# The last six row tiles of w2 straight into the result's bank, in four transfers, with the residual added by a matmul

## The chip, the cores and the metric

One core of one Trainium2 chip runs the kernel; the other cores stand idle. The metric is the device time of one execution in microseconds (us), and kernels are compared by the median of several executions. Beside that there is one profiled execution, whose trace gives a start and a duration for each instruction on each engine: PE is TensorE's matmul, PEld its weight load, DVE is VectorE, ACT ScalarE, POOL GpSimd, and SP the engine that issues the transfers here.

## The reference

One decode step of a parallel transformer block, for two sequences (B = 2) with one new token each, all in fp32. The layer norm of x feeds two branches, and the result is their sum with x:

```python
# x: (2, 1, 1024); k_cache, v_cache: (2, 4, 32768, 128)
# wq: (1024, 4096); wo: (4096, 1024); w1: (1024, 3584); w2: (3584, 1024)
xn = layernorm(x)
q = xn @ wq                                  # 32 query heads of 128, 4 key heads
p = softmax(q @ k.T * 128 ** -0.5)           # over 32768 cached positions
attn = (p @ v) @ wo
mlp = silu(xn @ w1) @ w2
return x + attn + mlp
```

Nearly all of the data are the two caches (2 x 4 x 32768 x 128 numbers each, 268 MB together) and the four weights; with two tokens, hardly any number read is used more than a few times.

## The kernel before

**The stream.** Everything large passes once through two SBUF buffers, `buf[0]` and `buf[1]`, of 128 partitions x 16384 fp32, 8 MiB each. `load` (line 169) issues a transfer on SP's queue, after a wait until the buffer's previous contents have been used. There are 40 steps (`STEPS`), alternating between the buffers: wq in two, w1 in two, then eight turns (4 key heads x 2 sequences) of two K halves and two V halves, then wo in two and w2 in two. All transfers come from SP in program order, so they stand in one queue.

**The matmuls of a step.** `slots(k, banks)` (line 300) works off a buffer with its 32 weights of 32 columns, `wt[k]`. A step is 32 matmul calls with 512 columns each; call (bank, r, q) goes to the 32 output partitions of column group q in one of two PSUM banks, and r = 0..3 accumulate. `ps[0]` and `ps[1]` are two banks each and together make `xy`. In fp32 a call shows as two matmul rows in the trace. A loop, `te_loop` (line 331), does a step on buffer A and then the first bank of a step on buffer B; a branch leads to `te_more` (line 338), which does the second bank and goes on to `te_k` or `te_v` and back, or, in the last of the 20 pairs, to `te_rest`. The semaphores `ld` (transfer landed) and `tok` (weights ready) are taken ahead of a step. `more[0]` and `more[1]` let a step wait for a second transfer in its middle: the last step of each buffer comes in pieces, and all other steps find enough counts there from the start (line 323).

**w2.** w2 has 28 row tiles of 128 rows x 1024 columns. The first sixteen go into buffer A in two transfers. The last twelve, tiles 0 to 11 in what follows, go into buffer B, in seven transfers (lines 185 to 187): tiles 0-5, tiles 6-7, tile 8, tile 9, tile 10, and tile 11 in a part with three quarters of each group's columns (`CUT`, 192 of 256) and one with the last quarter. Tiles 0 to 7 are worked off by `slots(1, (0,))` into the first bank of `ps[1]`: each r covers two tiles in halves of 512 columns, and r = 3, tiles 6-7, waits for `more[1]`. Tiles 8 to 11 go straight into `acc`, the bank of the result, by `tile` and `quarter` (lines 397 to 403): for each tile four calls of 256 columns, one per column group, on the semaphores `last[0]` to `last[4]`.

**How the result comes together.** ScalarE copies the banks of wo's two steps and w2's first step into `ev[0]` to `ev[2]` (line 254). POOL adds `ev[1]`, then x (`xs[:64, 256:768]`, line 380), then `ev[2]` (line 382); VectorE adds the two halves of that into `rest` (line 384), and then adds the first bank of `ps[1]` (line 386), which it may read after the PE semaphore's first mark, put on tile 8's last matmul. That gives `ob`, announced by `tob`. TensorE folds `ob` into `acc` with two matmuls against `fold` (lines 407 to 409), between tile 9 and tile 10. After tile 11, ScalarE copies `acc` to `ot` (line 256) and SP sends it out (line 389).

**What sets the order.** It is written out by hand: each engine runs its own instructions in program order, and semaphores tie them together. Matmuls all carry line 107 (the helper `mm`), transfers into the buffers line 172.

Of the kernel before, what the change touches and what calls it, by code (L numbers as in the profile page):

```python
# [8 lines left out]
B, HQ, HKV, SK, DH, D, F = 2, 32, 4, 32768, 128, 1024, 3584  # L9
P = 128  # L10
REP = HQ // HKV
W = 16384
NC = SK // W
KT = D // P
FT = F // P
QW = D // 4
CUT = 3 * QW // 4
LOOPS = HKV * B
STEPS = 4 + 4 * LOOPS + 4
PAIRS = STEPS // 2  # L20
# [31 lines left out]
def gqa_plus_mlp_kernel(nc, x8, kt, v0, v1, wq, wo, w1a, w1b, w2a, w2b, out):  # L52


    pe, dve, act, pool = (Stream(nc, e, n) for e, n in
                          ((nc.tensor, "pe"), (nc.vector, "dve"), (nc.scalar, "act"), (nc.gpsimd, "pool")))
    sp, T, V, A, G = nc.sync, nc.tensor, nc.vector, nc.scalar, nc.gpsimd
    sems = [pe.sem, dve.sem, act.sem, pool.sem]

    def sem(name):  # L60
        sems.append(nc.alloc_semaphore(name))
        return sems[-1]

    def sb(name, *shape):
        return nc.alloc_sbuf_tensor(name, shape, F32).ap()

    def bank(name, n=512):
        return nc.alloc_psum_tensor(name, (P, n), F32).ap()

    buf = [sb(n, P, W) for n in ("bufA", "bufB")]  # L70
    ld, more, tok = ([sem(f"{n}{k}") for k in "AB"] for n in ("ld", "more", "tok"))
    ldx, turn_sem = (sem(n) for n in ("ldx", "marks"))
    freed, subbed, normed, tq, pself = (sem(n) for n in ("freed", "subbed", "normed", "tq", "pself"))
    trm, tgd, tls, tob = (sem(n) for n in ("trm", "tgd", "tls", "tob"))
    last = [sem(f"last{i}") for i in range(5)]
    done = sem("done")

    weights, st = sb("weights", P, 64, 32), sb("st", P, 2048)
    wt = [weights[:, :32], weights[:, 32:]]
    xs, xT = sb("xs", P, D), sb("xT", P, KT, 32)  # L80
    stats, mv, ln = sb("stats", P, 2, V.BN_STATS_DIM), sb("mv", P, 2), sb("ln", P, 6)
    ev = [sb(f"ev{i}", P, 1024) for i in range(4)]
    sumq, sumh = sb("sumq", P, 1024), sb("sumh", P, FT * 32)
    tqs, qall = sb("tqs", P, 32, 32), sb("qall", P, LOOPS, REP)
    pre, sig, rsig = sb("pre", P, FT, 32), sb("sig", P, FT, B), sb("rsig", P, FT, B)
# [4 lines left out]
    def zeroed(*shape):  # L90
        n = shape[0] * (shape[1] if len(shape) > 1 else 1)
        lo = used[0]
        used[0] += n
        t = blank[:, lo:lo + n]
        return t.rearrange("p (a m) -> p a m", m=shape[1]) if len(shape) > 1 else t

    ident, sel, fold, rm, lsum, gd, ob = (zeroed(n) for n in (P, 32, 160, REP, REP, REP, 512))
    oT, hT = zeroed(HQ, 32), zeroed(FT, 32)
# [3 lines left out]
    ps = [xy[:, :1024], xy[:, 1024:]]  # L102
    smA, smB = bank("smA"), bank("smB")
    acc = bank("acc")[:, :QW]

    def mm(o, lhsT, rhs, start=True, stop=True):
        return T.matmul(o, lhsT, rhs, start=start, stop=stop)  # L107
# [13 lines left out]
    t = pool.mark(G.affine_select(out=ident, in_=ident, compare_op=ALU.not_equal, fill=1.0, base=0,  # L121
                                  pattern=[[-1, P]], channel_multiplier=1))
    pool.wait(t)
    halves = fold[:, 32:].rearrange("p (a m) -> p a m", m=64)[:, :, :32]
    t = pool.mark(G.tensor_add(halves, *(ident[:, 64 * g:64 * g + 64].rearrange("p (a m) -> p a m", m=32)
                                         for g in range(2))))
# [6 lines left out]
    for i in range(2):  # L133
        t = dve.mark(V.bn_stats(stats[:, i, :], xs[:, i * 512:(i + 1) * 512]))
    dve.wait(t)
    t = dve.mark(V.bn_aggr(mv, stats))
    var, std, y0, t0, t1, rstd = (ln[:, i:i + 1] for i in range(6))
    dve.wait(t)
    t = dve.mark(V.tensor_scalar_add(var, mv[:, 1:2], EPS))
    act.wait(t)  # L140
    t = act.mark(A.activation(std, var, AF.Sqrt))
    for f in (lambda: V.reciprocal(y0, std),
# [6 lines left out]
        t = dve.mark(f())  # L149
# [16 lines left out]
    def step(n):  # L166
        return (turn_sem, n) if n <= 2 else (freed, n - 2)

    def load(k, dst, src, s, n):
        if n:  # L170
            sp.wait_ge(*step(n))
        sp.dma_start(buf[k][:, dst] if isinstance(dst, slice) else dst, src).then_inc(s, 16)  # L172
# [3 lines left out]
    load(1, every, w1a, ld[1], 2)  # L176
    for it in range(LOOPS):
        h, b = divmod(it, B)
# [2 lines left out]
    load(0, every, wo[0], ld[0], STEPS - 5)  # L181
    load(1, every, wo[1], ld[1], STEPS - 4)
    load(0, slice(0, W // 2), w2a[:, :W // 2], ld[0], STEPS - 3)
    load(0, slice(W // 2, W), w2a[:, W // 2:], more[0], 0)
    cuts = [0, 6 * D, 8 * D, 9 * D, 10 * D, 11 * D, 11 * D + 4 * CUT, 12 * D]
    for lo, hi, s in zip(cuts, cuts[1:], [ld[1], more[1], *last]):
        load(1, slice(lo, hi), w2b[:, lo:hi], s, STEPS - 2 if lo == 0 else 0)


    for n in range(4):  # L190
        act.wait(step(n + 1))
        if n == 2:
            A.copy(ev[n][:, :512], ps[0][:, :512])
            A.copy(ev[n][:64, 512:], ps[0][:64, 512:])
            t = act.mark(A.copy(ev[n][64:96, 512:], ps[0][96:, :512]))
        else:
            t = act.mark(A.copy(ev[n], ps[n % 2]))
# [9 lines left out]
        elif n == 2:  # L207
            t = pool.mark(G.tensor_add(sumh[:96, 512:], a[:96, :384], b[:96, :384]))
            for j in range(3):
                pool.wait(t)  # L210
                t = pool.mark(G.tensor_add(sumh[96:, 512 + P * j:512 + P * (j + 1)], a[32 * j:32 * j + 32, 384:],
                                           b[32 * j:32 * j + 32, 384:]))
# [14 lines left out]
    t = dve.mark(V.transpose(pre.rearrange("p t m -> p (t m)"), sumh))  # L227

    act.wait(t)
    t = act.mark(A.activation(sig, pre[:, :, ::16], AF.Exp, scale=-1.0))  # L230
    for f in (lambda: V.tensor_scalar_add(sig, sig, 1.0), lambda: V.reciprocal(rsig, sig),
              lambda: V.tensor_mul(hT[:, :, ::16], pre[:, :, ::16], rsig)):
        dve.wait(t)
        t = dve.mark(f())
# [5 lines left out]
           tqs[:, :, ::16].rearrange("p (h m) b -> p h b m", m=REP)).then_inc(tq, 1)  # L240
    for it in range(LOOPS):
        h, b = divmod(it, B)
# [54 lines left out]
            m.then_inc(tok[c], 1)  # L297
        G.sem_inc(pself, -1)

    def slots(k, banks):  # L300

        m = None
        for bk in banks:
            for r in range(4):
                if (k, bk, r) in ((0, 1, 0), (1, 0, 3)):
                    pe.take(more[k], 16)
                for q in range(4):
                    e = 16 * bk + 4 * r + q
                    n = 16 * bk + 4 * q + r if k == 0 else e
                    m = mm(ps[k][32 * q:32 * q + 32, bk * 512:(bk + 1) * 512], wt[k][:, e, :],  # L310
                           buf[k][:, n * 512:(n + 1) * 512], r == 0, r == 3)
        return m

    def taken(k):
        pe.take(ld[k], 16)
        pe.take(tok[k])
# [3 lines left out]
    T.reg_mov(pair, 0)  # L320
    T.reg_mov(half, 0)
    pe.wait(i_const)
    for s, n in ((trm, 1), (tgd, 1), (tls, 1), (tob, 1), (more[0], 16 * PAIRS - 16), (more[1], 16 * PAIRS - 16)):
        T.sem_inc(s, n)
    T.br("te_loop")

# [4 lines left out]
    with nc.body("te_loop", valid_engines=engine):  # L331
        again = T.mark_branch_hint_location()
        taken(0)
        slots(0, (0, 1)).then_inc(turn_sem, 1)
        taken(1)
        slots(1, (0,))
        T.br_eq(pair, PAIRS - 1, on_true="te_rest", on_false="te_more")
    with nc.body("te_more", valid_engines=engine):
        slots(1, (1,)).then_inc(turn_sem, 1)
        T.reg_add(pair, pair, 1)  # L340
        T.br_eq(half, 0, on_true="te_k", on_false="te_v")
    with nc.body("te_k", valid_engines=engine):
# [6 lines left out]
    with nc.body("te_v", valid_engines=engine):  # L349
# [4 lines left out]
        for r in range(4):  # L354
            m = mm(smB[:, :REP], ob[:, r * P:(r + 1) * P], sel[:, REP * r:REP * (r + 1)], r == 0, r == 3)
        m.then_inc(turn_sem, 1)
        T.br("te_loop").branch_hint(again)
    with nc.body("turns", valid_engines=[V.engine, G.engine]):
        for eng, f, reg, step in turns:
            f()  # L360
            eng.reg_add(reg, reg, step)
            eng.br_lt(reg, step * LOOPS, on_true="turns", on_false="te_rest")
    nc.switch_bb("te_rest")
# [7 lines left out]
        G.tensor_copy(wt[c].rearrange("p (t d) m -> p t d m", d=2),  # L371
                      oT[:, 16 * c:16 * c + 16, None, :].to_broadcast([P, 16, 2, 32])).then_inc(tok[c], 1)
    pool.wait(i_hT)
    for c, n in enumerate((16, 8)):
        pool.wait(outs[c])
        G.tensor_copy(wt[c][:, :2 * n].rearrange("p (t d) m -> p t d m", d=2),
                      hT[:, 16 * c:16 * c + n, None, :].to_broadcast([P, n, 2, 32])).then_inc(tok[c], 1)
    t = pool.mark(G.tensor_add(ev[0], ev[0], ev[1]))
    pool.wait(t)
    t = pool.mark(G.tensor_add(ev[0][:64, :512], ev[0][:64, :512], xs[:64, 256:768]))  # L380
    pool.wait(t, outs[2])
    t = pool.mark(G.tensor_add(ev[0], ev[0], ev[2]))  # L382
    dve.wait(t)
    t = dve.mark(V.tensor_add(rest, ev[0][:, :512], ev[0][:, 512:]))  # L384
# [9 lines left out]
    sp.wait_ge(done, 16)  # L394
    sp.sem_inc(done, -16)

    def quarter(o, lhsT, w, start=False, stop=False):
        return [mm(o[32 * j:32 * j + 32, :], lhsT[j], w[j], start, stop) for j in range(4)][-1]

    def tile(t, o, lo, n, start=False, stop=False):  # L400
        T.wait_ge(last[t], 16)
        at = buf[1][:, lo:lo + 4 * n].rearrange("p (j n) -> p j n", j=4)
        return quarter(o, [hT[:, min(24 + t, FT - 1), :]] * 4, [at[:, j] for j in range(4)], start, stop)

    pe.mark(tile(0, acc, 8 * D, QW, True))
    tile(1, acc, 9 * D, QW)
    T.wait_ge(tob, 1)
    for c in range(2):
        mm(acc, fold[:, 32 - 32 * c:160 - 32 * c], ob[:, c * QW:(c + 1) * QW], False, False)
    tile(2, acc, 10 * D, QW)  # L410
    tile(3, acc[:, :CUT], 11 * D, CUT)
    pe.mark(tile(4, acc[:, CUT:], 11 * D + 4 * CUT, QW - CUT, False, True))


# [54 lines left out]
```

## Time and profile before

| | us |
|---|---|
| median of 3 runs | 772.55 |
| lowest and highest of them | 772.29 and 772.61 |
| profiled execution, its own time | 772.44 |
| span of its trace, first to last instruction | 771.1 |
| PE busy within the span | 392.9 |
| DVE, POOL, ACT busy | 133.3, 44.2, 29.0 |

The profiled execution spends 1.34 us around the span, so a time read from the trace stands to the execution's own time by that. Times in the trace count from the first instruction of the span. The mean granted TensorE clock was 0.752 of full speed. In rows of the timeline the first number is the start, the second the time that the group takes from first start to last end, "x" the number of instructions in the group, and the brackets say how long the engine was idle before and what released it. "PEq" is TensorE's own sequencer, "issue" idle time for which the profile shows no wait.

### The profile page before, as it was taken

The page shows a single profiled execution, that of the slowest core. Times are in us where ns is not written, and L with a number is a line of the kernel's source. Part 1 is how long each engine was busy: PE and PEld are TensorE (multiplying, and loading weights), DVE is VectorE, ACT ScalarE, POOL GpSimd, SP SyncE. Part 2 cuts the span into 40 slices and gives each one's busy share as a digit, 9 for nine tenths or more (in the row PEclk, how much of TensorE's full clock was granted, in tenths as well). Part 3 has the DMA queues.
Part 4 walks back from the last instruction along what each step waited for, and adds up shares of the span by engine and source line. Part 5 has one row for each costly group of instructions (what it writes and reads, how often), then busy time and mean ns, then how long its engine had stood idle before and what let it go on. Part 6 is the DMA issues. An engine that isn't in the chain of part 4 may idle for free. (4 is left out here: it accounts for less than half of the span.)

```text
span 771.1 us, 6114 instructions
## 1 busy us (share of the span) xinstructions
PE 392.9 (51%) x2702; PEld 125.9 (16%) x2702; DVE 133.3 (17%) x100; ACT 29.0 (4%) x39; POOL 44.2 (6%) x65
## 2 busy tenths in 40 slices
PE   0454554464545454645464545454645455545476
PEld 0111111121112111211121112111211121112122
DVE  2000104030403030304030303031303030313000
ACT  0000100100010001000100010001000100010000
POOL 3001200001000000010001000100010001000121
PEclk9977667767677767677767677767677767677689
DMA  9999999999999999999999999999999999999997
GB/s 382 435 435 435 435 435 435 435 435 435 435 435 435 435 435 435 435 435 435 435 435 435 435 432 435 425 428 418 425 432 435 432 435 435 435 435 435 435 433 329
DMA packets 6816, 331.40 MB, mean 430 GB/s; under 512 B 776, under 2 KB 920, under 8 KB 1440
## 3 DMA queue, kind: packets, MB, share of 16 engines
q1 hardware_dynamic: 6800, 331.37, 99.5%
q10 hardware_dynamic: 16, 0.03, 0.0%
HBM read 331.38 MB, written 0.02 MB: 430 GB/s over the span
## 5 line engine op out<-in xcount | busy, mean ns | idle before, releaser
L107 PE MATMUL xy<-bufB,weights 128*32 128x512 f32 x1248 | 181.8, 747 | 166.6 <-PEq L49 166.6
L107 PE MATMUL xy<-bufA,weights 128*32 128x512 f32 x1280 | 178.2, 718 | 100.4 <-PEq L49 100.4
L107 PEld LDWEIGHTS xy<-bufB,weights 128*32 128x32 f32 x1248 | 49.7, 134 | 298.8 <-issue 298.7
L107 PEld LDWEIGHTS xy<-bufA,weights 128*32 128x32 f32 x1280 | 49.9, 129 | 212.1 <-issue 212.1
L268 DVE STREAM_TRANSPOSE st<-xy 128x2048 f32<-128x2048 f32 x8 | 18.5, 2317 | 241.5 <-PE xy L107 241.5
L278 DVE TENSOR_REDUCE blank<-xy 128x512 f32<-128x2048 f32 x8 | 18.3, 2292 | 224.5 <-PE xy L107 224.5
L290 POOL MEMSET weights<- 128x2048 f32 x8 | 14.4, 1805 | 526.9 <-POOLq L49 526.9
L107 PE MATMUL smA<-blank 128*8 128x128 f32 x20 | 5.4, 370 | 51.9 <-PEq L49 51.9
L107 PE MATMUL smA<-blank,ones 128*128 128x8 f32 x18 | 4.9, 347 | 50.6 <-PEq L49 50.6
L269 DVE TENSOR_REDUCE blank<-st 128x8 f32<-128x2048 f32 x8 | 30.5, 3808 | 0.3
L279 DVE TENSOR_REDUCE blank<-weights 128x8 f32<-128x2048 f32 x8 | 30.4, 3798 | 0.0
L245 ACT ACTIVATE weights<-st 128x1024 f32<-128x1024 f32 x16 | 16.0, 1048 | 326.6 <-DVE st L275 326.6
L275 DVE TENSOR_TENSOR st<-st,gmax 128x2048 f32<-128x2048 f32 x8 | 18.3, 2292 | 0.3
L107 PE MATMUL smB<-blank 128*128 128x8 f32 x72 | 15.9, 349 | 0.0
L107 PEld LDWEIGHTS smB<-blank 128*128 128x128 f32 x72 | 15.6, 317 | 0.0
L107 PEld LDWEIGHTS smA<-blank,ones 128*128 128x128 f32 x18 | 4.3, 298 | 58.5 <-issue 58.5
L248 ACT COPY blank<-onew 128x8 f32<-128x8 f32 x8 | 1.6, 204 | 279.4 <-DVE onew L282 279.4
L107 PEld LDWEIGHTS smA<-blank 128*8 128x8 f32 x20 | 1.3, 89 | 60.2 <-issue 60.2
L384 DVE TENSOR_TENSOR rest<-ev 128x512 f32<-128x512 f32 x1 | 0.7, 693 | 49.1 <-POOL ev L382 49.1
L296 POOL COPY weights<-qall 128x128 f32 x32 | 8.0, 295 | 3.1 <-POOL weights L290 3.1
L107 PE MATMUL smB<-blank,ones 8*128 8x8 f32 x20 | 5.3, 333 | 5.7 <-PEq L49 5.7
L222 DVE STREAM_TRANSPOSE tqs<-sumq 128x1024 f32<-128x1024 f32 x1 | 1.2, 1245 | 38.2 <-POOL sumq L206 38.2
(59 smaller groups left out, 59.4 us busy)
## 6 DMA issues: line engine op xcount, KB each, us to landing
bufA<-in_w2a SPq DMA_DIRECT2D x2, 4096.0 KB, 24.0
bufA<-in_w1b SPq DMA_DIRECT2D x1, 6144.0 KB, 24.8
bufB<-in_w2b SPq DMA_DIRECT2D x1, 3072.0 KB, 16.5
bufB<-in_w2b SPq DMA_DIRECT2D x3, 512.0 KB, 20.2
bufB<-in_w2b SPq DMA_DIRECT2D x1, 1024.0 KB, 18.6
bufB<-in_w2b SPq DMA_DIRECT2D x1, 384.0 KB, 21.5
bufA<-in_kt SPq DMA_DIRECT2D x8, 27.7
bufB<-in_kt SPq DMA_DIRECT2D x8, 28.9
```

The lines of the kernel that those rows point to most:

```text
L107: return T.matmul(o, lhsT, rhs, start=start, stop=stop)
L222: i_q = dve.mark(V.transpose(tqs.rearrange("p c m -> p (c m)"), sumq))
L245: A.activation(wt[c].rearrange("p e m -> p (e m)"), st[:, 1024 * c:1024 * c + 1024], AF.Exp, scale=SCALE).then_inc(tok[c], 1)
L248: A.copy(oT[:, REP * h:REP * (h + 1), 16 * b], onew).then_inc(tq, 1)
L268: then(3, V.transpose(st, xy))
L269: V.tensor_reduce(rm, e8.rearrange("p n m -> p m n"), AX.X, ALU.max).then_inc(trm, 1)
L275: V.tensor_sub(e8, e8, gmax.to_broadcast([P, 256, REP])).then_inc(subbed, 1)
L278: V.tensor_reduce(ob, xy.rearrange("p (c n) -> p n c", c=4), AX.X, ALU.add).then_inc(tob, 1)
L279: V.tensor_reduce(lsum, weights.rearrange("p e (r m) -> p m (e r)", m=REP), AX.X, ALU.add).then_inc(tls, 1)
L290: G.memset(weights, 0.0).then_inc(pself, 1)
L296: m = G.tensor_copy(o, q[:, None, None, :].to_broadcast([P, 4, 4, REP]))
L384: t = dve.mark(V.tensor_add(rest, ev[0][:, :512], ev[0][:, 512:]))
```

## The change

The first bank of `ps[1]` gets only tiles 0-5 of the last twelve (r = 0 to 2), from the transfer of 3 MiB as before. In the place of r = 3 four matmuls add x to that bank: the identity's first 64 rows against `xs[:64, 256:768]`, one call per column group, and the PE semaphore's first mark moves to the last of these. POOL's addition of x goes. Tiles 6 to 11 all go into `acc` by calls of 256 columns, in four transfers (`PIECES`): tiles 6-8, tiles 9-10, and the two parts of tile 11 as before. The fold of `ob` stands behind tiles 6-8, ahead of tile 9. POOL spreads hT into six pairs of weights for this step rather than eight. `more` is one semaphore, for buffer A, and the wait in the middle of buffer B's steps is gone. In the loop the r = 3 calls move from `te_loop`, ahead of the branch, to `te_more`, behind it.

```diff
+PIECES = ((6, 9, 0, QW), (9, 11, 0, QW), (11, 12, 0, CUT), (11, 12, CUT, QW))
...
-    ld, more, tok = ([sem(f"{n}{k}") for k in "AB"] for n in ("ld", "more", "tok"))
+    ld, tok = ([sem(f"{n}{k}") for k in "AB"] for n in ("ld", "tok"))
+    more = sem("moreA")
...
-    last = [sem(f"last{i}") for i in range(5)]
+    last = [sem(f"last{i}") for i in range(len(PIECES))]
...
-    load(0, slice(W // 2, W), w2a[:, W // 2:], more[0], 0)
-    cuts = [0, 6 * D, 8 * D, 9 * D, 10 * D, 11 * D, 11 * D + 4 * CUT, 12 * D]
-    for lo, hi, s in zip(cuts, cuts[1:], [ld[1], more[1], *last]):
-        load(1, slice(lo, hi), w2b[:, lo:hi], s, STEPS - 2 if lo == 0 else 0)
+    load(0, slice(W // 2, W), w2a[:, W // 2:], more, 0)
+    load(1, slice(0, 6 * D), w2b[:, :6 * D], ld[1], STEPS - 2)
+    for (t0, t1, lo, hi), s in zip(PIECES, last):
+        at = slice(t0 * D + 4 * lo, (t1 - 1) * D + 4 * hi)
+        load(1, at, w2b[:, at], s, 0)
...
-    def slots(k, banks):
+    def slots(k, groups):
...
-        for bk in banks:
-            for r in range(4):
-                if (k, bk, r) in ((0, 1, 0), (1, 0, 3)):
-                    pe.take(more[k], 16)
-                for q in range(4):
-                    e = 16 * bk + 4 * r + q
-                    n = 16 * bk + 4 * q + r if k == 0 else e
-                    m = mm(ps[k][32 * q:32 * q + 32, bk * 512:(bk + 1) * 512], wt[k][:, e, :],
-                           buf[k][:, n * 512:(n + 1) * 512], r == 0, r == 3)
+        for bk, r in (divmod(g, 4) for g in groups):
+            if (k, bk, r) == (0, 1, 0):
+                pe.take(more, 16)
+            for q in range(4):
+                e = 16 * bk + 4 * r + q
+                n = 16 * bk + 4 * q + r if k == 0 else e
+                m = mm(ps[k][32 * q:32 * q + 32, bk * 512:(bk + 1) * 512], wt[k][:, e, :],
+                       buf[k][:, n * 512:(n + 1) * 512], r == 0, r == 3)
...
-    for s, n in ((trm, 1), (tgd, 1), (tls, 1), (tob, 1), (more[0], 16 * PAIRS - 16), (more[1], 16 * PAIRS - 16)):
+    for s, n in ((trm, 1), (tgd, 1), (tls, 1), (tob, 1), (more, 16 * PAIRS - 16)):
...
-        slots(0, (0, 1)).then_inc(turn_sem, 1)
+        slots(0, range(8)).then_inc(turn_sem, 1)
         taken(1)
-        slots(1, (0,))
+        slots(1, range(3))
         T.br_eq(pair, PAIRS - 1, on_true="te_rest", on_false="te_more")
     with nc.body("te_more", valid_engines=engine):
-        slots(1, (1,)).then_inc(turn_sem, 1)
+        slots(1, range(3, 8)).then_inc(turn_sem, 1)
...
-    for c, n in enumerate((16, 8)):
+    for c, n in enumerate((16, 6)):
...
-    t = pool.mark(G.tensor_add(ev[0][:64, :512], ev[0][:64, :512], xs[:64, 256:768]))
...
-    def quarter(o, lhsT, w, start=False, stop=False):
-        return [mm(o[32 * j:32 * j + 32, :], lhsT[j], w[j], start, stop) for j in range(4)][-1]
-
-    def tile(t, o, lo, n, start=False, stop=False):
-        T.wait_ge(last[t], 16)
-        at = buf[1][:, lo:lo + 4 * n].rearrange("p (j n) -> p j n", j=4)
-        return quarter(o, [hT[:, min(24 + t, FT - 1), :]] * 4, [at[:, j] for j in range(4)], start, stop)
-
-    pe.mark(tile(0, acc, 8 * D, QW, True))
-    tile(1, acc, 9 * D, QW)
-    T.wait_ge(tob, 1)
-    for c in range(2):
-        mm(acc, fold[:, 32 - 32 * c:160 - 32 * c], ob[:, c * QW:(c + 1) * QW], False, False)
-    tile(2, acc, 10 * D, QW)
-    tile(3, acc[:, :CUT], 11 * D, CUT)
-    pe.mark(tile(4, acc[:, CUT:], 11 * D + 4 * CUT, QW - CUT, False, True))
+    for q in range(4):
+        m = mm(ps[1][32 * q:32 * q + 32, :512], ident[:64, 32 * q:32 * q + 32], xs[:64, 256:768], False, True)
+    pe.mark(m)
+    first = True
+    for (t0, t1, lo, hi), s in zip(PIECES, last):
+        T.wait_ge(s, 16)
+        for t in range(t0, t1):
+            at = buf[1][:, t * D + 4 * lo:t * D + 4 * hi].rearrange("p (j n) -> p j n", j=4)
+            for j in range(4):
+                m = mm(acc[32 * j:32 * j + 32, lo:hi], hT[:, 16 + t, :], at[:, j], first, hi == QW and t == 11)
+            first = False
+        if t1 == 9:
+            T.wait_ge(tob, 1)
+            for c in range(2):
+                mm(acc, fold[:, 32 - 32 * c:160 - 32 * c], ob[:, c * QW:(c + 1) * QW], False, False)
+    pe.mark(m)
```

## The prediction

> **What bounds the kernel now.** I read the page first: the DMA rows say whether anything but the transfers can matter, then the chain of waits says where the end is set.
>
> ```profile
> span 771.1 us, 6114 instructions
> DMA  9999999999999999999999999999999999999997
> GB/s 382 435 435 435 435 435 435 435 435 435 435 435 435 435 435 435 435 435 435 435 435 435 435 432 435 425 428 418 425 432 435 432 435 435 435 435 435 435 433 329
> q1 hardware_dynamic: 6800, 331.37, 99.5%
> bufA<-in_v SPq DMA_DIRECT2D x8, 27.1
> bufB<-in_v SPq DMA_DIRECT2D x8, 28.9
> ```
>
> The DMA engines are busy in every slice, at 435 GB/s in most. 331.37 MB at 435 GB/s are 761.8 us of a span of 771.1. The two last rows are the time from issue to landing of full buffers of 8 MiB (8.39 MB). Streaming one takes 8.39 / 435 = 19.3 us, so a load is queued 7.8 to 9.6 us before the stream needs it. TensorE could be some microseconds later in any loop turn without a hole in the stream. So only the tail can change, and I go to the chain in order of time and the timeline there.
>
> ```profile
> 744.37 0.33 SPq L172
> 744.74 0.44 SPq L172
> 745.22 0.43 SPq L172
> 745.69 20.18 DMA bufB<-in_w2b
> 765.92 2.94 PE acc L107 x36
> 768.89 0.37 ACT ot L256
> ```
>
> The chain names one transfer of w2, the fourth issued (tile 9, landed 745.69 + 20.18 = 765.87), and then 2.94 us of matmuls in one piece. That piece hides other waits, so I take the issues one by one and the timeline.
>
> ```profile
> bufB<-in_w2b SPq DMA_DIRECT2D x1, 3072.0 KB, 16.5
> bufB<-in_w2b SPq DMA_DIRECT2D x1, 1024.0 KB, 18.6
> bufB<-in_w2b SPq DMA_DIRECT2D x1, 512.0 KB, 19.4
> bufB<-in_w2b SPq DMA_DIRECT2D x1, 512.0 KB, 21.0
> bufB<-in_w2b SPq DMA_DIRECT2D x1, 384.0 KB, 21.5
> 746.17 0.91 SPq L172 DMA_DIRECT2D bufB<-in_w2b  x2
> 746.64 0.91 SPq L172 DMA_DIRECT2D bufB<-in_w2b  x2
> bufB<-in_w2b SPq DMA_DIRECT2D x1, 128.0 KB, 21.3
> ```
>
> Issue plus time to landing gives when each piece is there: tiles 0-5 at 744.37 + 16.5 = 760.87; tiles 6-7 at 763.34; tile 8 at 764.62; tile 9 at 765.87; tile 10 at 746.17 + 21.0 = 767.17; the wide part of tile 11 at 746.64 + 21.5 = 768.14; the narrow part at about 747.11 + 21.3 = 768.41.
>
> ```profile
> 761.11 3.64 PE L107 MATMUL xy<-bufB,weights 128*32 128x512 f32 x32 [2.13 <-PEq L49]
> 761.54 0.15 PEld L107 LDWEIGHTS xy<-bufB,weights 128*32 128x32 f32 x4 [0.28 <-issue]
> 761.97 0.16 PEld L107 LDWEIGHTS xy<-bufB,weights 128*32 128x32 f32 x4 [0.27 <-issue]
> 762.59 0.69 DVE L384 TENSOR_TENSOR rest<-ev 128x512 f32<-128x512 f32 x1 [49.12 <-POOL ev L382]
> 764.64 0.64 PE L107 MATMUL acc<-bufB,blank 128*32 128x256 f32 x8
> 765.42 0.69 DVE L386 TENSOR_TENSOR blank<-rest,xy 128x512 f32<-128x512 f32 x1 [2.14 <-PE acc L107]
> 765.92 0.64 PE L107 MATMUL acc<-bufB,blank 128*32 128x256 f32 x8 [0.64 <-DMA bufB<-in_w2b]
> 766.49 1.13 PE L107 MATMUL acc<-blank 128*128 128x256 f32 x4
> 767.24 0.38 PE L107 MATMUL acc<-blank 128*128 128x256 f32 x1
> 767.55 1.27 PE L107 MATMUL acc<-bufB,blank 128*32 128x256 f32 x24
> 768.17 0.48 PEld L107 LDWEIGHTS acc<-bufB,blank 128*32 128x32 f32 x16 [0.47 <-DMA bufB<-in_w2b]
> ```
>
> Prices from these rows. Sixteen calls make 32 matmul rows, so a call is two passes. Weight loads come in fours every 0.43 us: four 512-column passes, one per 32-column group, go side by side in 0.43 us. By columns, four 256-column passes take 0.215, and a row tile into the result's bank (two passes, four groups) takes 0.43. Alone it shows 0.64, so 0.21 is the fill at the end. The 24 rows at 767.55 check this: 0.43 for tile 10, 0.32 for 192 columns, 0.11 for 64, 0.21 of fill make 1.07; the row says 1.27, and the missing 0.20 is the wait that the weight loads show: tile 10 was through at 767.98, the next weights loaded at 768.17, 0.03 after the landing at 768.14. So the end is set now by the wide part of tile 11: 768.17 + 0.32 + 0.11 + 0.21 = 768.81, the 768.82 of the trace. After that come ACT and the output transfer, which the change leaves alone.
>
> **The change part by part.** *Transfers.* The bytes and their order stay; two transfers fewer. Landing to landing, 1024 KB took 763.34 − 760.87 = 2.47 us, three of 512 KB took 767.17 − 763.34 = 3.83, or 1.28 each. Two 512s cost 2.55 against 2.47 for one of 1024, so a merge saves 0.08 us. Two merges: tiles 6-8 land at 760.87 + 2.47 + 1.28 − 0.08 = 764.54, tiles 9-10 at 767.01, the wide part of tile 11 at 767.98, the narrow one at 768.25. That is 0.16 sooner. Bounds: 0, if the merged transfers run at the old pace; 0.31, if the last 3.15 MB ran at 435 GB/s (7.23 us, not 768.41 − 760.87 = 7.54). A loss has no ground, with the same bytes in fewer pieces. SP's two saved issues (some 0.47 each, at 745 to 747) are worth nothing: the queue has work until 753.6, where the first matmuls on w2a's second half start:
>
> ```profile
> 753.65 5.33 PE L107 MATMUL xy<-bufA,weights 128*32 128x512 f32 x32 [5.32 <-PEq L49]
> 748.48 1.25 POOL L380 TENSOR_TENSOR ev<-ev,xs 64x512 f32<-64x512 f32 x1
> 760.20 2.36 POOL L382 TENSOR_TENSOR ev<-ev 128x1024 f32<-128x1024 f32 x1 [10.46 <-ACT ev L254]
> ```
>
> *POOL's residual add* (1.25 us) goes, and its weight copy spreads six tiles, not eight. Both are worth nothing: POOL sat idle for 10.46 us behind that add until ScalarE had copied the next bank, and `rest` is there at 763.28, before anything needs it.
>
> *The loop.* In each of 20 pairs, r = 3 of the first bank moves behind the branch, and a wait with its decrement goes. Nothing is queued behind it that the stream waits for: the cover is the 7.8 us worked out above; without it a delay would be paid in full.
>
> *TensorE in the tail.* The r = 3 group (four calls of 512 columns, 0.86 us) is replaced by the residual: four calls of 512 columns, too, but with 64 rows under them. The trace shows no such shape. Low bound: packed by fours as its neighbours, 2 × 0.43 = 0.86. High bound: one pass after another, 8 × 0.43 = 3.44. I take 0.86, since it differs from the nearest rows only in its row count and the four outputs lie in four groups as theirs do. Changing shape has a price: from the last fold matmul at 767.24 to tile 10's at 767.55 are 0.31, of which 256 columns take 0.21, so 0.10. Bounds: 0, and 0.54 from a turn of the loop where the next weights came 0.97 after the previous ones instead of 0.43 (a jump to another block lies in it too):
>
> ```profile
> 84.43 0.13 PEld L107 LDWEIGHTS xy<-bufB,weights 128*32 128x32 f32 x4 [0.29 <-issue]
> 84.86 0.13 PEld L107 LDWEIGHTS xy<-bufB,weights 128*32 128x32 f32 x4 [0.29 <-issue]
> 85.83 0.30 PEld L107 LDWEIGHTS smA<-blank,ones 128*128 128x128 f32 x2 [0.84 <-issue]
> ```
>
> Here a rule of the Trainium skill speaks against the change. Its page TensorEngine Tiling (Array Packing), section Key Properties, says that a change of tiling mode, not only of tile, drains the TensorE; its section Available Configurations lists 64-row and 128-row shapes as different modes. By that rule the residual pays two drains. The trace agrees at the fold with the 0.10 above; if a drain cost the whole fill of 0.21, the sum would be 0.22 later.
>
> Then tiles 6 and 7 cost a second time, in another form: 2 × 0.43 = 0.86 new in the result's bank, behind the residual. The sum on TensorE, from 761.11:
> - r = 0 to 2, six groups of 0.43: 763.69.
> - Switch and residual, 0.10 + 0.86: 764.65; switch back: 764.75. Tiles 6-8 landed at 764.54, so no wait.
> - Tiles 6-8, 1.29: 766.04. Meanwhile the residual's end (764.65 + 0.21) releases DVE, which took 0.14 to start (764.64 + 0.64 to 765.42) and 0.69 to run: `ob` at 765.69, so the new place of the fold, ahead of two tiles instead of one tile and a wait, does not wait for it.
> - Fold: from tile 9's last issue (765.92 + 0.43 = 766.35) to tile 10's start at 767.55 it took 1.20, of which 0.14 (766.35 to 766.49) may have been the wait for DVE. I take 1.20, low bound 1.06: 767.24. Tiles 9-10 landed at 767.01.
> - Tiles 9-10, 0.86: 768.10. The wide part of tile 11 landed at 767.98: 0.32 → 768.42; the narrow part 0.11 and the fill 0.21 → 768.74.
>
> So TensorE comes 0.12 after the transfers, where it used to wait 0.20 for them: the work moved eats nearly all that the merged transfers give. 768.74 against 768.82 is −0.08 us. The profiled execution had 772.44 (1.34 around its span); the median of the runs is 772.55, 0.11 above it. Forecast: 772.36 on the profiled scale, 772.5 on the median's.
>
> **The rivals.** A change of 0.2% (1.55 us) is about what a measurement of this kernel can tell from none.
>
> *The transfers give all and TensorE keeps up.* All 0.31 is gained, the fold takes 1.06 and switches cost nothing: TensorE would be through at 768.74 − 0.34 = 768.40, the landing allows 768.14 − 0.31 + 0.03 + 0.64 = 768.50. That is −0.32: 772.2. For it, 435 GB/s elsewhere; against it, the switch seen at the fold.
>
> *TensorE is later than the sum.* Five 256-column tiles at the 0.64 of a tile alone: 5 × 0.21 = +1.05, so 773.5. Or the jump into the last block, now ahead of the residual, is not covered: +0.54, so 773.0. Against the first: 1.27 us for the last 24 rows only fits with overlap. Against the second: the sequencer has all of r = 0 to 2 in hand once tiles 0-5 have landed, 2.6 us of matmuls to hide the jump under. The page Runtime: NRT & Kernel Launch of the Trainium skill, section Instruction fetch mechanics, has a taken branch to a page not at hand wait for its fetch; the gap at 85.83 may be one, no row here separates it.
>
> *The residual does not pack* (the other side). If the 64-row passes go one after another, 3.44 replace 0.86. From 763.69 on TensorE waits for no landing, so every microsecond is paid: 768.74 + 2.58 = 771.32, that is 772.5 + 2.6 = 775.1, slower by 0.3%. It decides from a residual of about 0.86 + 0.08 + 1.55 = 2.5 us. For it: nothing but that no row has this shape; against it: the neighbours' packing.
>
> *The clock drops.* The rows of stages show it granted at 0.50 after 5.32 us without matmuls and at 1.00 after the 2.13 us ahead of tile 0:
>
> ```profile
> 754.00:755.00 1.00, 1.00 (x8) 0.26 (x4) 0.00 (x0) 0.00 (x0) 0.00 (x0) 0.50 0.91 393
> 762.00:763.00 1.00, 1.00 (x16) 0.44 (x12) 0.41 (x1) 0.00 (x0) 0.56 (x1) 1.00 0.97 397
> ```
>
> The change leaves both gaps, so I give it 1 in 100; at half speed the 7.6 us from 761.11 double, some 780 us.
>
> **How the numbers follow.** Forecast of 772.5 (within 0.3): 0.64. Transfers give all, 772.2: 0.10. TensorE late, 773.0 to 773.5: 0.16. Residual unpacked, 775.1: 0.06. Clock: 0.01. Gains in the loop that no row shows: 0.03. The first three lie within 0.2%, so no change has 0.89 with a little taken off each way; slower 0.08, faster 0.03. Range 772.0 to 773.5: from 0.2 under the fullest gain of the transfers to the worst of the late TensorE; it leaves out about 1 in 10.
>
> **What would show it.** Right: five transfers of w2b, the last landing 0.1 to 0.2 sooner; weight loads of the residual in fours, 0.43 apart, where r = 3 stood; the DVE add starting about 765.0 instead of 765.42; no DMA wait ahead of tile 11, and ScalarE's last copy at 768.8 as before. Wrong: eight residual passes in single file; a gap ahead of the residual; tiles at 0.64 each; a landing no sooner, or half clock after 761; any hole in the stream before 753.

## The result: 3.5 us slower, and not within the span

The changed kernel takes 776.0 us (775.82 to 776.15), the kernel before 772.53 beside it: a ratio of 1.0046, 95% interval 1.0033 to 1.0059. The forecast was 772.5 and the range ended at 773.5. Yet the page of the changed kernel shows the same span and the same stream as before:

```profile
span 771.2 us, 6122 instructions
DMA  9999999999999999999999999999999999999997
q1 hardware_dynamic: 6512, 331.37, 99.4%
```

Its profiled execution took 776.15 us. The kernel before had 772.44 − 771.1 = 1.34 us outside the span; here it is 776.15 − 771.2 = 4.95. All the time lost lies outside what the page describes, and the two spans differ by 0.1 us.

First the span. The tail of the timeline of the changed kernel (start, time of the group; line 109 is the matmul helper now):

```profile
761.23 2.78 PE L109 MATMUL xy<-bufB,weights 128*32 128x512 f32 x24 [1.37 <-PEq L50]
763.94 1.06 PE L109 MATMUL xy<-xs,blank 64*32 64x512 f32 x8
764.93 1.50 PE L109 MATMUL acc<-bufB,blank 128*32 128x256 f32 x24
765.14 0.69 DVE L387 TENSOR_TENSOR blank<-rest,xy 128x512 f32<-128x512 f32 x1 [0.93 <-PE xy L109]
766.36 1.13 PE L109 MATMUL acc<-blank 128*128 128x256 f32 x4
767.42 1.51 PE L109 MATMUL acc<-bufB,blank 128*32 128x256 f32 x32
769.00 0.37 ACT L259 COPY ot<-acc 128x256 f32<-128x256 f32 x1 [8.06 <-PE acc L109]
```

The residual's 64-row matmuls run packed by fours: eight rows in 1.06 us, of which 0.21 is the fill. TensorE goes on without a wait for a landing to 767.42 + 1.51 = 768.93, 0.11 later than before. The chain of waits, which named a transfer before, is TensorE alone now, up to ScalarE's copy:

```profile
761.18 0.04 issue
761.23 3.77 PE xy L109 x32
765.00 3.98 PE acc L109 x60
768.98 0.02 issue
769.00 0.37 ACT ot L259
```

The issues' times to landing, with the first issue at 743.53:

```profile
743.53 2.23 SPq L174 DMA_DIRECT2D bufB<-in_w2b  x5
bufB<-in_w2b SPq DMA_DIRECT2D x1, 3072.0 KB, 17.4
bufB<-in_w2b SPq DMA_DIRECT2D x1, 1536.0 KB, 20.7
```

Tiles 0-5 land at 743.53 + 17.4 = 760.93. By the trace's semaphore events the other pieces follow at 764.63, 767.11, 768.11 and 768.39. From the first landing to the last are 7.45 us; before, 768.42 − 760.82 = 7.60.

Now what lies behind the span. The view of the transfers can be asked for a stretch past the last instruction. From 772 to 777 us it shows this for the changed kernel:

```profile
DMA packets 1, 0.02 MB, mean 3 GB/s; under 512 B 0, under 2 KB 0, under 8 KB 0
q8 instruction: 1, 0.02, 1.7%
```

and this for the kernel before:

```profile
DMA packets 0, 0.00 MB, mean 0 GB/s; under 512 B 0, under 2 KB 0, under 8 KB 0
```

One transfer of 16,384 bytes of *instructions* starts at 772.58 and takes 1.33 us. The semaphore events in the trace show what waits for it. Behind the program semaphore 2 changes from 771.20 to 771.37 and again from 772.20 to 772.56 in the kernel before, and from 771.31 to 771.97 nearly all others change once, in five runs of numbers. I read this as a barrier of the engines, a reset of all semaphores, each engine its share, and a second barrier. The shares of four engines are done by about 771.8 in both kernels. The fifth, semaphores 7 to 53, is reset from 771.63 to 771.97 before the change, and from 775.37 to 775.70 with it. The last event before the change is at 772.56, with it at 776.28.

### The profile page after: what moved, and what is told of

It is laid out like the page before. It is cut to its first block, busy times and chain, and to the rows that moved or that the text cites. A ratio compares the mean times of both kernels' runs of the same rounds, so it can differ in the third digit from the quotient of the medians.

```text
span 771.2 us, 6122 instructions
## 1 busy us (share of the span) xinstructions
PE 387.9 (50%) x2718; PEld 125.2 (16%) x2718; DVE 133.3 (17%) x100; ACT 29.0 (4%) x39; POOL 42.8 (6%) x64
## 5 line engine op out<-in xcount | busy, mean ns | idle before, releaser
L109 PE MATMUL xy<-bufB,weights 128*32 128x512 f32 x1240 | 173.0, 720 | 169.6 <-PEq L50 169.6
L109 PE MATMUL xy<-bufA,weights 128*32 128x512 f32 x1280 | 180.4, 726 | 103.2 <-PEq L50 103.2
L109 PEld LDWEIGHTS xy<-bufB,weights 128*32 128x32 f32 x1240 | 48.1, 130 | 294.5 <-issue 294.5
## 6 DMA issues: line engine op xcount, KB each, us to landing
bufB<-in_w2b SPq DMA_DIRECT2D x1, 3072.0 KB, 17.4
```

## The experiments

Theory: TensorE's program has grown past a limit, so that its end has to be fetched. Compiled, it has 26,112 bytes before and 29,056 with the change. A call is four rows of the trace (two weight loads, two matmuls); 12 calls added 3,072 bytes, so a row is an instruction of 64 bytes, and the programs have 408 and 454 of them. The other four engines' programs have less than 4,000 bytes each, and idle calls appended to TensorE's leave them as long as they were. The rivals were the two semaphores fewer, the transfers, and the executed matmuls themselves.

**Twelve idle calls behind the last matmul of the kernel before:**

```diff
     pe.mark(tile(4, acc[:, CUT:], 11 * D + 4 * CUT, QW - CUT, False, True))
+    for i in range(12):
+        mm(smA[32 * (i % 4):32 * (i % 4) + 32, :64], hT[:, FT - 1, :], ident[:, :64])
```

> The kernel before, with 12 matmul calls of 64 columns that serve nothing appended to TensorE's program behind its last matmul (into the idle bank smA): 456 instructions of 64 bytes in TensorE's program instead of 408; the changed kernel has 454. They run under the output's transfer, so the span should stay at 771.1. Theory of the program's length: a 16 KB fetch of instructions behind the span and about 776.0 us. Theories of the semaphores or of the transfers (both are as before here): 772.5 and no such fetch.

Measured: 774.16 us, ratio 1.0023 (1.0014 to 1.0033), with the fetch, but not where any theory had put it. The span grew to 772.6. The transfers from 768 to 776 us:

```profile
q8 instruction: 1, 0.02, 1.0%
out_y<-ot SPq DMA_DIRECT2D x1, 16.0 KB, 3.4
```

and in the kernel before:

```profile
out_y<-ot SPq DMA_DIRECT2D x1, 16.0 KB, 1.7
```

The fetch starts at 770.20 here, beside the output's transfer, which takes 3.4 us instead of 1.7. Fifteen of that transfer's sixteen completions come by 770.90, and one at 772.53. The packet of that piece starts at 771.43, just as the fetch ends (770.20 + 1.25): the fetch lies in the way of one piece of the output. Length costs time without a change in the transfers or the semaphores, but how much depends on when TensorE runs out.

**The same calls where no branch ever goes:**

```diff
-        T.br("te_loop").branch_hint(again)
+        T.br_eq(half, 0, on_true="te_loop", on_false="te_pad").branch_hint(again)
+    with nc.body("te_pad", valid_engines=engine):
+        for i in range(12):
+            mm(smA[32 * (i % 4):32 * (i % 4) + 32, :64], hT[:, FT - 1, :], ident[:, :64])
+        T.br("te_loop")
```

> The kernel before, with the same 12 calls in a block of TensorE's program that no branch ever takes (458 instructions): nothing more is executed than one compare in a branch per turn. If the length of the program counts, whether or not it is executed: about 776.0 and the 16 KB fetch. If executed instructions count: 772.5.

Measured: 773.31 us, 1.0012 (1.0002 to 1.0022). Not the 776, yet the fetch is there, at 769.32, and the output takes 2.4 us to land:

```profile
q8 instruction: 1, 0.02, 0.9%
out_y<-ot SPq DMA_DIRECT2D x1, 16.0 KB, 2.4
```

These calls are never executed, so it is the place of the end in the program that counts.

**The transfers without the longer program:** tiles 6-7 stay in the other bank, POOL adds x, five transfers.

```diff
-    cuts = [0, 6 * D, 8 * D, 9 * D, 10 * D, 11 * D, 11 * D + 4 * CUT, 12 * D]
-    for lo, hi, s in zip(cuts, cuts[1:], [ld[1], more[1], *last]):
+    cuts = [0, 6 * D, 9 * D, 11 * D, 11 * D + 4 * CUT, 12 * D]
+    for lo, hi, s in zip(cuts, cuts[1:], [ld[1], more[1], *last[2:]]):
...
-        T.wait_ge(last[t], 16)
+        if t >= 2:
+            T.wait_ge(last[t], 16)
...
     pe.mark(tile(0, acc, 8 * D, QW, True))
-    tile(1, acc, 9 * D, QW)
     T.wait_ge(tob, 1)
...
+    T.wait_ge(last[2], 16)
+    tile(1, acc, 9 * D, QW)
     tile(2, acc, 10 * D, QW)
```

> The kernel before with w2's last twelve tiles in the change's five transfers, and the fold ahead of tile 9 as in the change; tiles 6-7 stay with r = 3 in the other bank and POOL adds x as before (TensorE's program 408 instructions, as before). Theory of the program's length: no fetch behind the span; the span alone moves, since r = 3 now waits for tiles 6-8 at about 764.6: r = 3 and tile 8 to 765.9, VectorE to 766.9, fold to 768.1, four tiles' worth to 769.5, some 0.7 us more, 773.2. Theory of the transfers: 776 or more, with some 3.5 us outside the span.

Measured: 773.16 us, 1.0009 (1.0000 to 1.0019), span 772.1, no fetch. The transfers cost nothing outside the span. Inside it, r = 3 waits for tiles 6-8, and VectorE and the fold are late behind it. The time is the 773.2 worked out; in the profiled execution the steps come up to 0.3 us later than expected (VectorE's add ends at 767.19, not 766.9):

```profile
764.87 1.06 PE L107 MATMUL xy<-bufB,weights 128*32 128x512 f32 x8 [0.76 <-PEq L49]
766.50 0.69 DVE L386 TENSOR_TENSOR blank<-rest,xy 128x512 f32<-128x512 f32 x1 [2.16 <-PE acc L107]
767.25 1.13 PE L107 MATMUL acc<-blank 128*128 128x256 f32 x4 [0.88 <-DVE blank L386]
768.31 1.51 PE L107 MATMUL acc<-bufB,blank 128*32 128x256 f32 x32
```

So this is also what the change avoids by moving tiles 6 and 7 out of that bank.

**The changed kernel with as many semaphores as before:**

```diff
+    spare = [sem(f"spare{i}") for i in range(2)]
     done = sem("done")
```

> The changed kernel with two semaphores more that nothing uses, so that as many stand in the range that is cleared as in the kernel before. Theory of the semaphores: back to 772.5. Theory of the program's length (454 instructions as in the changed kernel): 776.0 with the fetch.

Measured: 775.79 us, 1.0043 (1.0026 to 1.0060), span 771.0, the fetch at 772.52. The semaphores are not it.

**A longer program that should be faster:** two idle calls behind the changed kernel's last matmul.

```diff
     pe.mark(m)
+    for i in range(2):
+        mm(smA[32 * i:32 * i + 32, :64], hT[:, FT - 1, :], ident[:, :64])
```

> The changed kernel with two of the idle matmul calls behind its last one: 462 instructions in TensorE's program, 8 more than the changed kernel. If what costs is that TensorE runs out of fetched instructions only behind the closing barrier (as in the changed kernel, where the 16 KB fetch starts at 772.58, after the others are through), a longer program runs out sooner, ahead of that barrier and beside the output's transfer, as with 12 calls added to the kernel before: 773.3 to 774.3, faster than the changed kernel though it does more. If each added instruction just costs, 776 or more.

Measured: 773.89 us, 1.0019 (1.0010 to 1.0029): 2.1 us less than the changed kernel, with more to do. The timeline shows TensorE running out in the middle of the idle calls:

```profile
768.48 0.17 PEld L109 LDWEIGHTS smA<-blank 128*32 128x32 f32 x2
768.53 0.22 PE L109 MATMUL smA<-blank 128*32 128x64 f32 x1
771.69 0.30 PE L109 MATMUL smA<-blank 128*32 128x64 f32 x3 [2.94 <-issue]
771.69 0.14 PEld L109 LDWEIGHTS smA<-blank 128*32 128x32 f32 x2 [3.04 <-issue]
```

Two weight loads and one matmul, then nothing for 2.94 us, for which the profile names no other engine; the fetch starts at 769.28 in that gap. Here TensorE is caught before the barrier, and the gap lies beside the output's transfer.

**Where the limit is:** 8, 4, 10 and 11 idle calls behind the kernel before, with the edit of the twelve, and the changed kernel made shorter.

> The kernel before with 8 idle matmul calls behind TensorE's last one: 440 instructions. If the limit is a place in TensorE's program that 454 instructions meet at the closing reset of the semaphores, 440 meet it some 14 resets later: a fetch behind the span and 775 to 776, the span as before. If the cost grows with the length (0 at 408, 3.5 at 454): about 774.9. If a limit lies between 440 and 454: 772.4.

> The kernel before with 4 idle calls: 424 instructions. Same place met 30 resets later: the fetch behind the span, 775 to 776. Cost in proportion to the length: 773.6. A limit above 424: 772.4, and no fetch.

> The kernel before with 10 idle calls: 448 instructions in TensorE's program. The limit lies between 442 (772.4) and 454 (776.0). In the changed kernel with 8 more instructions TensorE stood still after 3 of those 8, so 457 of its own fit ahead of the closing instructions; with some 4 to 6 of these, 448 should still fit: 772.4, no fetch. If the limit is 448 or less: 775 to 776.

> The kernel before with 11 idle calls: 452 instructions. By the same count TensorE reaches its end inside the closing instructions, behind the barrier as the changed kernel does: 775.5 to 776, span 771.1, one fetch of 16 KB behind it. If 452 still fits: 772.4.

```diff
-    for q in range(4):
-        m = mm(ps[1][32 * q:32 * q + 32, :512], ident[:64, 32 * q:32 * q + 32], xs[:64, 256:768], False, True)
-    pe.mark(m)
+    pe.mark(mm(ps[1][:, :512], ident[:64, :], xs[:64, 256:768], False, True))
```

> The changed kernel with the residual in one call of 128 columns of weights instead of four of 32, 442 instructions. The residual costs TensorE the same 0.86 us (two passes of 512 columns one after another), so the span stays at 771.0 to 771.2. A place met later in the resets: 775 to 776; a limit between 442 and 454: 772.4.

| kernel | TensorE's program, instructions | span, us | time, us | fetch starts at |
|---|---|---|---|---|
| before | 408 | 771.1 | 772.4 to 772.5 | none |
| before + 4 calls | 424 | 771.0 | 772.36 | none |
| before + 8 calls | 440 | 771.1 | 772.33 | none |
| changed, residual in one call | 442 | 771.1 | 772.43 | none |
| before + 10 calls | 448 | 771.1 | 772.55 | none |
| before + 11 calls | 452 | 771.1 | 775.73 | 773.10 |
| changed | 454 | 771.2 | 776.00 | 772.58 |
| changed, two semaphores more | 454 | 771.0 | 775.79 | 772.52 |
| before + 12 calls | 456 | 772.6 | 774.16 | 770.20 |
| before + 12 calls never run | 458 | 771.6 | 773.31 | 769.32 |
| changed + 2 calls | 462 | 772.0 | 773.89 | 769.28 |
| before, five transfers | 408 | 772.1 | 773.16 | none |
| before + 40 calls never run (below) | 570 | 776.5 | 778.27 | 766.98, 770.24 |

The expectation that 440 and 424 would meet the limit some resets later was wrong: the events of the resets are not an instruction each. Up to 448 nothing happens. At 452, ratio 1.0043 (1.0027 to 1.0060), TensorE's resets are done on time (771.59 to 771.94) and the barrier behind them is late (775.65 instead of some 772.2); the stretch from 771 to 777 us shows the fetch:

```profile
q8 instruction: 1, 0.02, 1.1%
```

At 454 the resets are late, too. From 456 to 462 TensorE is caught ahead of the first barrier, and part of the wait is hidden under the output. So the fetch costs 3.3 to 3.5 us when only the last few instructions are missing, and 0.9 to 1.8 when some more are.

The changed kernel with the residual in one call is the change's own test: the same transfers, the same order, 12 instructions fewer. It takes 772.43 us, a ratio of 1.0001 (0.9992 to 1.0011). Its residual and its last tiles:

```profile
763.77 1.12 PE L109 MATMUL xy<-xs,blank 64*128 64x512 f32 x2
764.82 1.02 PEld L109 LDWEIGHTS acc<-bufB,blank 128*32 128x32 f32 x24 [0.76 <-DMA bufB<-in_w2b]
766.25 1.13 PE L109 MATMUL acc<-blank 128*128 128x256 f32 x4
767.32 1.51 PE L109 MATMUL acc<-bufB,blank 128*32 128x256 f32 x32
```

**Running out in the middle of the work:** 40 calls in the block that is never taken, by the edit of the twelve never run with `range(40)`.

> The kernel before with 40 idle calls in a block that is never taken, 570 instructions, so that the whole last block of TensorE's program (tile 8 on) lies behind the limit. The fetch then comes when TensorE jumps there, about 763.5 to 764.5, with the data stream still running, instead of at the end; by the 2.4 to 3.5 us from running out to going on seen so far tile 8 starts at 766.5 to 767.5 instead of 764.6, and tile 8, 9, VectorE's add, fold, tiles 10-11 follow: 774.0 to 775.0. If the fetch is hidden under the third group's matmuls: 772.5 to 773.

Measured: 778.27 us, 1.0079 (1.0063 to 1.0096), span 776.5. It is worse than the 774 to 775 expected. The chain of waits and the timeline:

```profile
760.99 3.64 PE xy L107 x32
764.63 4.93 issue
769.57 1.93 PE acc L107 x16
```

```profile
769.57 0.20 PEld L107 LDWEIGHTS acc<-bufB,blank 128*32 128x32 f32 x8 [5.84 <-issue]
771.53 1.67 PE L107 MATMUL acc<-blank 128*128 128x256 f32 x4
```

TensorE stands for 4.93 us at the jump into its last block. The fetch starts only at 766.98, while the stream's last transfers still run; with an empty queue TensorE went on after 2.94. In the whole span there are two fetches:

```profile
q8 instruction: 2, 0.03, 0.0%
```

The second one, at 770.24, takes 0.96 us and costs nothing that shows: TensorE's matmuls go on from 769.57 to 771.50 without a gap. The second part of the loss is speed: the fold takes 1.67 instead of 1.13 us, and the stage's clock is lower (busy time and rows of PE, PEld, DVE, ACT and POOL, then the granted clock, the DMA engines' share and GB/s):

```profile
764.00:769.50 5.50, 0.63 (x8) 0.00 (x0) 0.19 (x1) 0.00 (x0) 0.00 (x0) 0.98 0.69 265
769.50:774.00 4.50, 4.40 (x44) 2.31 (x44) 0.69 (x1) 0.00 (x0) 0.00 (x0) 0.65 0.01 4
```

## Why the prediction was wrong

The step that failed is the last line of the sum: "The profiled execution had 772.44 (1.34 around its span)". The time around the span was carried over as a constant, its change put at nothing without a reason. It measured 4.95 with the change, and 1.3 to 1.6 in each kernel without a fetch. The part-by-part costs counted what TensorE's added calls take to run, and not what they add to the program: 12 calls are 48 instructions, less two that belonged to the wait that went, and with 454 the closing of the program no longer fits. The kernels with 448 and 452 instructions, 772.55 and 775.73 us, show that step of the cost without the change. No rival held this. The nearest was the jump into the last block, priced +0.54; the kernel with 40 calls never run shows that such a jump costs 4.93 us once its target lies behind the limit, but in the change it does not, and only 0.13 us stand ahead of the residual. The gap at 85.83, which the prediction thought might be a fetch, is none: the span before holds no instruction transfer at all.

The rest of the sum can be read from the kernel with the residual in one call, where nothing lies behind the span: 772.43 against a forecast of 772.5, and a ratio of 1. A time so near to no change would agree with several of the rivals, so the terms say more than the sum. In the changed kernel:

- *Transfers:* right. The last landing comes 0.15 us sooner counted from the first (7.45 against 7.60); forecast 0.16. It is no accident of one execution: the eight kernels with seven pieces show 7.60 to 7.63, the five with five pieces 7.45 to 7.49.
- *Residual packed:* right, 1.06 us with the fill; the unpacked rival falls. One sign came otherwise than written: the residual's eight weight loads stand together in 0.15 us at 763.94, not in fours 0.43 apart. By columns, one call of 128 columns of weights costs nearly the same, 1.12, in a quarter of the instructions; the 12 that it saves are what matters.
- *Switches:* 0.13 each, not 0.10. The matmuls of r = 2 should be through at 761.23 + 6 × 0.43 = 763.81, and the residual starts at 763.94; that at 764.80, and the tiles start at 764.93. The rule of the Trainium skill that was weighed (TensorEngine Tiling (Array Packing), Key Properties: a change of mode drains the TensorE) agrees so far as each change costs time, some 0.6 of the fill and not all of it.
- *VectorE's add:* 765.14 instead of "about 765.0".
- *Fold:* 1.20 was right: tiles 6-8 are issued by 764.93 + 3 × 0.43 = 766.22, and tiles 9-10 start at 767.42. The reading that 0.14 of it may have been the wait for VectorE was not. The same 0.14 stands ahead of the fold here, from 766.22 to 766.36, with VectorE through at 765.14 + 0.69 = 765.83; before, too, VectorE was through at 765.42 + 0.69 = 766.11, ahead of tile 9's last issue at 766.35. So the low bound of 1.06 was too low, and this 0.14 comes with the switch to the fold's shape.
- *TensorE comes after the transfers:* right. No row behind 764.93 waits visibly for a landing, and the end at 768.93 is 0.19 past the forecast of 768.74, 0.12 of it from a first matmul at 761.23 instead of 761.11 and 0.06 from the two switches.
- *Loop, POOL, clock:* as forecast: the stream has no hole, and the clock is granted in full from 761 on. POOL's last add starts 0.9 us later than before (761.10), but `rest` is there at 763.52 + 0.69 = 764.21, still ahead of its use at 765.14.

The page Runtime: NRT & Kernel Launch of the Trainium skill, section Instruction fetch mechanics, says that programs are fetched in blocks of 16 KiB and that crossing into a new one is mostly hidden. The size agrees with the 16,384 bytes here. That it is hidden holds here for one fetch, the second with 40 calls never run, and not for the others: 3.3 to 3.5 us at the end of the program, 4.93 ahead of the last block.

## What to carry to other kernels

Compare the execution's own time with its span before explaining a difference by any instruction in it: where the spans agree and the times don't, look for transfers behind the last instruction. A program's length is a cost of its own with a step in it, so an edit that unrolls or adds calls is to be counted in instructions, too, and the cheapest mend may be the same work in fewer calls (here one matmul call instead of four). Where the step can't be avoided, the place at which the engine runs out decides: here it cost least beside a transfer that had to be waited for anyway (0.9 to 1.8 us), and most at the very end (3.3 to 3.5) or ahead of the critical work (4.93).

## What had not been expected of the hardware

- The limit for TensorE's program in this kernel lies above 448 and at or below 452 instructions. An estimate from the gap with 2 calls more puts the place itself at 454 + 3 = 457 instructions after the start, since three of the added eight ran ahead of it. This fits the table: at 452 and 454 there is room for 5 and 3 instructions of the closing, at 456 for 1, and at 448 for 9, which is enough. How many instructions the runtime puts before the kernel's own was not measured, nor whether the other engines have the same limit. That the fetch is TensorE's follows from its program alone being lengthened and from its gaps; the trace names no engine.
- A fetch takes 0.9 to 1.3 us once it moves, but TensorE stands 2.9 to 4.9 us where its gap can be seen. Part of that lies behind the transfer: in all seven kernels with a fetch, the late matmul, reset or barrier comes 1.5 to 1.6 us after the transfer's end (with the change 772.58 + 1.33 = 773.91, and the reset at 775.37). Why it takes that long, and why the fetch starts so late, 1.1 us behind the barrier's last event (771.47) in the changed kernel, stays open.
- Beside a fetch of 16 KB, a transfer of 16 KB came late in all three kernels where they met: one of its sixteen completions 1.6, 0.6 and 0.4 us after the others. Only in the first is the late packet seen to start as the fetch ends; in the other two the packets moved on time, and why one completion was late stays open.
